# Turning normalized blocks on TensorE in a layer of sliding-window attention and routed experts

## The chip, the cores and the metric

The kernel runs on one core of one Trainium2 chip. The core has four engines that compute: TensorE (PE in the profile, its weight loads PEld), VectorE (DVE), ScalarE (ACT) and GpSimd (POOL). SyncE (SP) issues nearly all transfers, and 16 DMA engines carry them. The metric is the device time of one execution in microseconds (us), as the median of several runs.

## The reference

One transformer layer on 2048 tokens of 512 features, all in float32. A layer norm goes ahead of attention (32 heads of 16 features, each query sees the last 256 keys), a second one ahead of a mixture of 8 experts, of which each token uses two. Cut to what matters:

```python
def _A_ref(x, wqkv, wo):                    # H = 32, Dh = 16, W = 256
    q, k, v = split_heads(x @ wqkv)
    scores = einsum("bhqd,bhkd->bhqk", q, k) * (Dh ** -0.5)
    mask = (i - j >= 0) & (i - j < W)
    p = softmax(where(mask, scores, -1e9))
    return merge_heads(einsum("bhqk,bhkd->bhqd", p, v)) @ wo

def _B_ref(x, wg, w1, w2):                  # E = 8, F = 1376, K = 2
    gates = softmax(x @ wg); the two largest, scaled to sum 1 -> cw
    h = gelu(einsum("nd,edf->nef", x, w1))
    return einsum("ne,ned->nd", cw, einsum("nef,efd->ned", h, w2))

h  = x + _A_ref(layernorm(x), wqkv, wo)
h2 = h + _B_ref(layernorm(h), wg, w1, w2)
```

## The kernel before

The tokens are worked in four chunks of 512 (c = 0 to 3), each of four blocks of 128. Matrix products run in a split form: each float32 operand becomes a high part (a cast on ScalarE, line 361) and a low part (source minus high part, on VectorE, line 363, or GpSimd, line 365), and three products are added up (high by high, high by low, low by high).

For each chunk `norm_and_v` normalizes the four blocks, turns them so that features lie on partitions (the tiles `xh`, `xl`), and makes V (line 482). `qk` makes queries and keys for 8 groups of 4 heads (u = 8c + g, line 535), splits the result, writes it to DRAM (`qkd`, lines 547 to 549) and reads it back in another layout (lines 555 and 560). `maxes` computes scores for the row maxima (lines 588 to 606; the maxima go through DRAM as `md`, lines 609 and 612), and `attend` the probabilities (lines 636 to 660) and their product with V (line 676). `project` scales and projects (line 748), adds the residual (line 815), normalizes again (lines 806 and 822), writes the normalized rows to `xnd` in DRAM and computes gate logits (line 851); `route` picks two experts per token and scatters table entries. Then `experts` runs the 8 experts (lines 1118 and 1139) from about 665 us on.

How a block is turned is what the change touches. TensorE turns 128 x 128 pieces through an identity, four per block, into one PSUM bank: for chunk 0 ahead of Q, K and V (line 466), for the last chunk ahead of the gate (line 839), and in the experts (line 1090). For chunks 1 to 3 ahead of Q, K and V, and for chunks 0 to 2 ahead of the gate, the kernel goes another way: normalized rows are written to DRAM (`xd`, line 450, or `xnd`, which is written anyway), read back with 32 x 32 pieces arranged by partition (line 454 into `xz`, line 829 into `oz`), and VectorE transposes inside 32 x 32 squares (lines 472 and 844). In that form the features stand in another order, so the weights `wqkv` are loaded in the same order by `rows_of`, whose DRAM pattern has the slowest dimension 4, then 32 rows, then the columns (lines 392 and 387), and the gate weights exist twice (`wgt[0]`, `wgt[1]`).

The order on each engine is not that of the code. Each piece of work is a task of a planner (`Plan`) with an engine, a planned duration, a priority (about the number of the group it belongs to) and buffers; `Plan.order` walks through a planned time and emits the tasks, and each engine then runs its instructions strictly in that order, waiting where one is not ready. SP too issues its transfers in one row. There are 7 PSUM banks for general use (`single`, printed as one_74 to one_80 in the instruction order, `one` in the trace); `mr`, `mf` and `zone` are large SBUF tiles in which nearly all named pieces lie.

Of the kernel before, what the change touches and what calls it, by code (L numbers as in the profile page):

```python
# [155 lines left out]
def layer(tc, x, wqkv, wo, wg, w1, w2, out):  # L156
# [55 lines left out]
    xt_t = [take(mf, 512) for _ in range(2)]  # L212
# [70 lines left out]
    wgt = [const([128, 4, E], F32, f"wgt{i}") for i in range(2)]  # L283
# [61 lines left out]
    def rows_of(w, c, cols=slice(None)):  # L345
# [7 lines left out]
                     h=NH, n=NN, nt=1, xt=2, y=2, osl=1, ohl=2, ahead=2))  # L353
# [51 lines left out]
    def norm_and_v(c):  # L405
# [6 lines left out]
        zb = []  # L412
# [23 lines left out]
        for b in range(4):  # L436
            def norm(b=b):
                t = xn[xb[b].h]
                if c == 0:
                    nc.vector.tensor_scalar(xt_t[zb[b].h].rearrange("p (c q i) -> p c q i", c=4, q=4),  # L440
                                            t.rearrange("p (q c i) -> p c q i", c=4, q=4),
                                            mv["v"][:, b, 0:1], mv["y"][:, b:b + 1], op0=OP.subtract, op1=OP.mult)
                else:
                    nc.vector.tensor_scalar(t, t, mv["v"][:, b, 0:1], mv["y"][:, b:b + 1], op0=OP.subtract, op1=OP.mult)
            if c == 0:
                zb.append(Buf("xt"))
                nb.append(add("DVE", 456, norm, [rs[b]], p + 0.5, [xb[b], zb[b]]))
# [9 lines left out]
        xT, vd = [], []
        for b in range(4):
            pp = p + 1.0 + b * 0.2
            s = slice(b * 128, (b + 1) * 128)  # L460
            if c == 0:
                bk = Buf("one")

                def turn(b=b, bk=bk):
                    for k in range(4):
                        nc.tensor.transpose(single[bk.h][:, k * 128:(k + 1) * 128], xt_t[zb[b].h][:, k * 128:(k + 1) * 128], ident)
                tr = add("PE", 872, turn, [nb[b]], pp, [zb[b], bk])
                xT += split(pp, lambda s=s: xh[:, :, s], lambda s=s: xl[:, :, s],
                            lambda bk=bk: single[bk.h].rearrange("p (k t) -> p k t", k=4), [tr], [bk])
            else:  # L470
                tb = Buf("xt")
# [807 lines left out]
```

## Time and profile before

| | |
|---|---|
| median of 3 runs | 1244.97 us (1242.53 to 1249.09) |
| the profiled execution, its own time | 1246.75 us |
| span of its trace, first to last instruction | 1244.7 us |
| TensorE busy | 1118.5 us, 90% of the span |
| VectorE, ScalarE, GpSimd busy | 678.2, 540.8, 455.1 us |
| granted TensorE clock, mean | 0.948 of full speed |

Busy time is the union of an engine's instructions, so that an engine can be busy all the time with short overlaps and still not stream at its peak. The granted clock is the share of its full 2.4 GHz that TensorE was given; 0.5 is 1.2 GHz. Three stretches have to be read apart: 0 to 40 us, in which TensorE does almost nothing but turn four blocks; 40 to 705 us, the attention and routing of four chunks; and 705 us to the end, the experts, in which TensorE is busy nearly without a gap.

### The profile page before, as it was taken

To read this page: it belongs to the slowest core of one execution; us is meant where nothing else is said; L and a number is where in the kernel's file an instruction comes from. 1 tells how busy PE (TensorE), PEld (TensorE's weight loads), DVE (VectorE), ACT (ScalarE), POOL (GpSimd) and SP (SyncE) were. 2 spreads that over 40 slices of the span, in tenths; PEclk is the share of its full clock that TensorE was granted. 3 is DMA by queue.
4 is the path that set the end of the run, shared out by engine and by line. 5 is a ranking of instruction groups with operands and counts; after the bars stand their busy time and mean duration, and the time that the engine had idled before them with its cause. 6 is when DMAs were issued, how large, how long until landed. Compare 5 with 4: busy or idle time off the path is not lost.

```text
span 1244.7 us, 19621 instructions
## 1 busy us (share of the span) xinstructions
PE 1118.5 (90%) x6801; PEld 892.2 (72%) x6801; DVE 678.2 (54%) x1833; ACT 540.8 (43%) x1153; POOL 455.1 (37%) x668
## 2 busy tenths in 40 slices
PE   1797989979898999998788999999999999999994
PEld 0574666657666676766357889889798897989893
DVE  4288567977787786776546144434243342434341
ACT  1335555434554445544555245425253351626240
POOL 4734544744556464653844411220302112020101
PEclk9998998999899898996887899999999999999997
DMA  3489799884799758777332634442534334353422
GB/s 114 112 239 274 207 243 275 252 197 89 190 260 263 179 120 213 197 214 183 108 118 75 144 104 123 113 82 89 120 115 122 87 107 87 105 130 112 105 66 29
DMA packets 111617, 185.51 MB, mean 149 GB/s; under 512 B 25092, under 2 KB 44612, under 8 KB 111508
## 3 DMA queue, kind: packets, MB, share of 16 engines
q1 hardware_dynamic: 102852, 166.42, 47.7%
q0 software_dynamic: 8656, 17.73, 7.7%
q8 instruction: 56, 0.92, 0.3%
q14 instruction: 53, 0.43, 0.1%
HBM read 124.51 MB, written 59.60 MB: 148 GB/s over the span
## 4 chain that ended last, share of the span: by engine, by line
PE 67%; DMA 17%; DVE 6%; SPq 3%; POOL 2%; issue 2%; ACT 1%; POOLq 0%; DVEq 0%; ACTq 0%
PE one L1139 21%; PE one L1118 21%; PE one L588 5%; PE one L535 5%; PE oT L676 4%; PE one L636 4%; DMA mr<-qkd 3%; PE one L748 2%; PE one L482 2%; DMA md<-mt 2%; DMA mr<-md 2%; DMA od<-zone 1%; PE one L851 1%; SPq L387 1%; DVE mx L597 1%
## 5 line engine op out<-in xcount | busy, mean ns | idle before, releaser
L640 ACT ACTIVATE zone<-one 128x384 f32<-128x384 f32 (+1 forms) x480 | 207.8, 494 | 155.2 <-PE one L636 131.7
L1118 PE MATMUL one<-mr 128*128 128x256 f32 (+7 forms) x1980 | 269.2, 298 | 0.0
L1118 PEld LDWEIGHTS one<-mr 128*128 128x128 f32 (+1 forms) x1980 | 266.7, 188 | 1.1
L1139 PE MATMUL one<-zone,mr 128*128 128x512 f32 (+3 forms) x1080 | 260.4, 397 | 0.0
L660 POOL TENSOR_SCALAR_AFFINE_SELECT zone<-zone 128x256 f32<-128x256 f32 (+1 forms) x368 | 169.5, 483 | 201.4 <-ACT zone L640 198.8
L1139 PEld LDWEIGHTS one<-zone,mr 128*128 128x128 f32 (+3 forms) x1080 | 193.3, 181 | 53.0
L363 DVE TENSOR_TENSOR mr<-one,mr 128x256 fp32r<-128x256 f32 (+9 forms) x205 | 100.5, 494 | 180.1 <-ACT mr L361 171.2
L597 DVE TENSOR_REDUCE mx<-one 128x1 f32<-128x256 f32 (+2 forms) x472 | 192.3, 426 | 0.8
L588 PE MATMUL one<-mr 126*128 126x384 f32 (+2 forms) x512 | 166.1, 376 | 19.9 <-DMA mr<-qkd 10.7
L636 PE MATMUL one<-mr 128*128 128x384 f32 (+1 forms) x592 | 152.9, 336 | 21.1 <-DMA mr<-md 11.2
L594 DVE COPY_PREDICATED one<-above,one 128x128 f32<-128x128 uint32 x448 | 120.8, 289 | 77.3 <-PE one L588 68.7
L588 PEld LDWEIGHTS one<-mr 126*128 126x128 f32 x512 | 95.7, 201 | 78.1 <-issue 25.9
L636 PEld LDWEIGHTS one<-mr 128*128 128x128 f32 x592 | 109.6, 204 | 48.6 <-DVE mx L597 17.0
L361 ACT CAST mr<-one 128x256 fp32r<-128x256 f32 (+9 forms) x205 | 87.6, 431 | 128.8 <-PE one L1090 113.6
L1085 POOL DMA_INDIRECT mf<-xnd,tb x36 | 35.1, 975 | 287.6 <-PE one L1090 271.4
L535 PE MATMUL one<-mr 128*128 128x512 f32 x384 | 108.8, 413 | 23.2 <-ACT mr L361 23.0
L361 ACT CAST mr<-mf 128x512 fp32r<-128x512 f32 (+4 forms) x120 | 93.2, 787 | 82.2 <-DMA mf<-in_B_w_dram 26.1
L1123 ACT ACTIVATE one<-one 128x256 f32<-128x256 f32 (+7 forms) x165 | 65.2, 395 | 142.7 <-PE one L1118 132.6
L1145 DVE TENSOR_SCALAR mf<-one,tb 128x512 f32<-128x512 f32 (+3 forms) x36 | 27.0, 750 | 173.2 <-PE one L1139 173.2
L1147 POOL DMA_INDIRECT out_dram<-mf,tb x36 | 61.5, 1708 | 162.2 <-DVE mf L1145 142.6
L676 PE MATMUL oT<-zone 128*17 128x384 f32 (+2 forms) x1408 | 110.9, 407 | 8.1 <-POOL zone L660 6.9
L365 POOL TENSOR_TENSOR mr<-mf,mr 128x512 fp32r<-128x512 f32 (+2 forms) x74 | 94.1, 1284 | 55.4 <-ACT mr L361 50.6
(141 smaller groups left out, 965.6 us busy)
## 6 DMA issues: line engine op xcount, KB each, us to landing
mf<-in_B_w_dram SPq DMA_DIRECT2D x32, 688.0 KB
mf<-in_B_w_dram SPq DMA_DIRECT2D x40, 512.0 KB
qkd<-mr SPq DMA_DIRECT2D x32, 512.0 KB
mr<-qkd SPq DMA_DIRECT2D x80, 192.0 KB
mr<-qkd SPq DMA_DIRECT2D x48, 288.0 KB
mr<-wgd SPq DMA_DIRECT2D x24, 512.0 KB
mf<-in_A_x_dram SPq DMA_DIRECT2D x32, 256.0 KB
qkd<-mr SPq DMA_DIRECT2D x64, 128.0 KB
```

Source lines behind the costliest of these rows:

```text
L361: a = add("ACT", 51 + n * 0.86, lambda: nc.scalar.copy(dst_h(), src()), deps, prio, bufs)
L363: b = add("DVE", 65 + n * 1.05, lambda: nc.vector.tensor_sub(dst_l(), src(), f32(dst_h())), [a], prio, bufs)
L535: nc.tensor.matmul(single[bk.h], wt()[:, int(i == 1), k * 128:(k + 1) * 128], xt[:, k], start=(i == 0 and k == 0), stop=(i == 2 and k == 3))
L588: nc.tensor.matmul(view()[:, j], Q[slot.h][0:126, h + j, b * 128:(b + 1) * 128], K[slot.h][0:126, (h + j) // 2, (b + k0) * 128:(b + 3) * 1 ...
L594: nc.vector.copy_predicated(t[:, :, n - 128:n], above.unsqueeze(1).to_broadcast([128, m, 128]), src)
L597: nc.vector.tensor_reduce(mx_t[slot.h][:, h:h + m, b], view()[:, :, max(0, n - 256):n], axis=AX.X, op=OP.max)
L636: nc.tensor.matmul(single[bk.h][:, off:off + w], K[slot.h][:, h // 2, r * 128:(r + 1) * 128], Q[slot.h][:, h:h + hs, b * 128:(b + m) * 128 ...
L640: return add("ACT", 51 + n * 0.833, lambda: nc.scalar.activation(dst(), single[bk.h][:, 0:n].rearrange(order, q=128, **({"h": 2} if "h" in ...
L660: nc.gpsimd.affine_select(v, v, pattern=[[0, v.shape[1]], [-1 if far else 1, 128]], compare_op=OP.is_gt if far else OP.is_ge, fill=0.0, ba ...
L676: nc.tensor.matmul(oT[32 * j:32 * j + 17, b * 128:(b + n) * 128], V[blk % NV][:, 4 * g + j, :], PT[pt.h][j // 2][:, off:off + n, j % 2], s ...
L1118: nc.tensor.matmul(bank(), a[:, k, f * 128:f * 128 + w], b[:, k, :n], start=(i == 0), stop=(i == 11))
L1139: nc.tensor.matmul(single[bk.h][:n], h[a][:w], spot["w2"][b][f][:w], start=(f == 0 and q == 0), stop=(f == NF - 1 and q == 2))
```

## The change

All blocks are now turned by TensorE, out of the normalized tile itself: chunks 1 to 3 ahead of Q, K and V (line 454 of the new kernel; for chunk 0 it was so), and chunks 0 to 2 ahead of the gate (line 811). The bounces through `xd` and back from `xnd`, and the 32 x 32 transposes, are gone. After a turn the high part is cast out of PSUM on ScalarE, as before, and the low part comes from VectorE, not GpSimd; ahead of the gate ScalarE copies the turned block to `nt_t`. The features keep their order, so `wqkv` is loaded as plain blocks of 128 rows. The columns for the first four groups of Q and K (half 0) are loaded first, then those of V, then half 1. There is one `wgt`. The priority of the gate's turn is now that of its block, not of the chunk.

```diff
-    wqk_in = [dma(lambda k=k: nc.sync.dma_start(wqk[:, k], rows_of(wqkv, k, slice(0, 1024))), 524288, [], -9) for k in range(4)]
+    wqkv_rows = wqkv.rearrange("(k p) n -> p k n", p=128)
+    def wqk_half(k, i):
+        def cols(a):
+            return a.rearrange("p (s i n) -> p s i n", s=2, i=2)[:, :, i]
+        nc.sync.dma_start(cols(wqk[:, k]), cols(wqkv_rows[:, k, 0:1024]))
+    wqk_in = [[dma(lambda k=k, i=i: wqk_half(k, i), 262144, [], -9 if i == 0 else -2.9) for k in range(4)] for i in range(2)]
     for k in range(4):
-        load_split(k, rows_of(wqkv, k, slice(1024, 1536)), (wvh, wvl), k, -3, wv_done, "POOL" if k < 4 else "DVE")
+        load_split(k, wqkv_rows[:, k, 1024:1536], (wvh, wvl), k, -3, wv_done, "POOL")
...
-                a = add("DVE", 456, norm, rs, p + 0.5, [xb[b]])
-                nb.append(dma(lambda b=b: nc.sync.dma_start(xd[c][b * 128:(b + 1) * 128], xn[xb[b].h]), 262144, [a], p + 0.5, [xb[b]]))
-        if c > 0:
-            zr = []
-            for f in range(4):
-                zr.append(dma(lambda f=f: nc.sync.dma_start(
-                    xz[f * 32:(f + 1) * 32].rearrange("p (t c) -> p t c", c=128),
-                    ap(xd[c], f * 128, [[512, 32], [16384, 16], [1, 128]])), 262144, nb, p + 0.6, xb))
+                nc.vector.tensor_scalar(t, t, mv["v"][:, b, 0:1], mv["y"][:, b:b + 1], op0=OP.subtract, op1=OP.mult)
+            nb.append(add("DVE", 456, norm, [rs[b] if c == 0 else rs[0]], p + 0.5, [xb[b]]))
...
-                tr = add("DVE", 610, lambda b=b, tb=tb: nc.vector.transpose(
-                    xt_t[tb.h].rearrange("p (k t j) -> p t k j", k=4, t=4),
-                    xz[:, b * 512:(b + 1) * 512].rearrange("p (t k i) -> p t k i", t=4, k=4)), zr, pp, xb + [tb])
-                xT += split(pp, lambda s=s: xh[:, :, s], lambda s=s: xl[:, :, s], lambda tb=tb: xt_t[tb.h].rearrange("p (k t) -> p k t", k=4),
-                            [tr] + free_x, [tb], lo="POOL")
+            bk = Buf("one")
+            def turn(b=b, bk=bk):
+                for k in range(4):
+                    nc.tensor.transpose(single[bk.h][:, k * 128:(k + 1) * 128], xn[xb[b].h][:, k * 128:(k + 1) * 128], ident)
+            tr = add("PE", 440, turn, [nb[b]] + free_x, pp, [xb[b], bk])
+            xT += split(pp, lambda s=s: xh[:, :, s], lambda s=s: xl[:, :, s],
+                        lambda bk=bk: single[bk.h].rearrange("p (k t) -> p k t", k=4), [tr], [bk])
...
-                      lambda: wqk.rearrange("p k (s g c) -> p k s g c", s=2, g=8)[:, :, :, g], wqk_in, wsb, lo="DVE" if g < 0 else "POOL")
+                      lambda: wqk.rearrange("p k (s g c) -> p k s g c", s=2, g=8)[:, :, :, g], wqk_in[g // 4], wsb, lo="DVE" if g < 0 else "POOL")
...
-        if not end:
-            for f in range(4):
-                zr.append(dma(lambda f=f: nc.sync.dma_start(
-                    oz[f * 32:(f + 1) * 32].rearrange("p (t c) -> p t c", c=128),
-                    ap(xnd, (512 * c + 128) * 512 + f * 128, [[512, 32], [16384, 16], [1, 128]])), 262144,
-                    [xn_done[4 * c + b] for b in range(4)], p + gap, [zs]))
...
-                cp = add("DVE", 610, lambda b=b: nc.vector.transpose(
-                    nt_t.rearrange("p k (t j) -> p t k j", t=4), oz[:, b * 512:(b + 1) * 512].rearrange("p (t k i) -> p t k i", t=4, k=4)),
-                    zr, pb, [zs, tb])
+            pb = p + 0.7 + 0.3 * b if end else p + step * b + 0.9
+            tb, bk = Buf("nt"), Buf("one")
+            def turn(bk=bk, nb=nbs[b]):
+                for k in range(4):
+                    nc.tensor.transpose(single[bk.h][:, k * 128:(k + 1) * 128], n_t[nb.h][:, k * 128:(k + 1) * 128], ident)
+            tr = add("PE", 440, turn, [norms[b]], pb, [bk, nbs[b]])
+            cp = add("ACT", 478, lambda bk=bk: nc.scalar.copy(nt_t, single[bk.h].rearrange("p (k t) -> p k t", k=4)), [tr], pb, [bk, tb])
```

ScalarE at the start, before. `one_74` is the bank of the first turned block, the `mf` sources are columns of Q and K weights, the `zone` sources the V weights.

```order
L361 CAST mr<-one_74 128x4x128
L361 CAST mr<-mf 128x512 x2
L361 CAST mr<-zone 128x512 x2
L361 CAST mr<-one_75 128x4x128
L361 CAST mr<-zone 128x512
L361 CAST mr<-one_76 128x4x128
L361 CAST mr<-zone 128x512
L361 CAST mr<-one_77 128x4x128
L361 CAST mr<-mf 128x512 x6
```

Each turned block stood behind one more piece of V weights. ScalarE at the start, now:

```order
L360 CAST mr<-mf 128x512 x2
L360 CAST mr<-zone 128x512 x2
L360 CAST mr<-one_74 128x4x128
L360 CAST mr<-zone 128x512 x2
L360 CAST mr<-mf 128x512 x2
L360 CAST mr<-one_75 128x4x128
L360 CAST mr<-one_76 128x4x128
L360 CAST mr<-one_77 128x4x128
L360 CAST mr<-mf 128x512 x4
```

The casts of the first four groups' weights and of V now stand ahead of the last three blocks.

GpSimd at the start, now: low parts of weights (`mf` for Q and K, `zone` for V), zeroing of the Q and K tiles (lines 406 and 407) and of a column in the V tiles (408); the two low parts at the end hold that of the first group's queries and keys.

```order
L364 TENSOR_TENSOR mr<-mf,mr 128x512
L406 MEMSET mr 128x2048
L407 MEMSET mr 128x1536
L364 TENSOR_TENSOR mr<-mf,mr 128x512
L364 TENSOR_TENSOR mr<-zone,mr 128x512 x3
L364 TENSOR_TENSOR mr<-mf,mr 128x512
L364 TENSOR_TENSOR mr<-zone,mr 128x512
L406 MEMSET mr 128x2048
L408 MEMSET zone 128x32 x10
L407 MEMSET mr 128x1536
L364 TENSOR_TENSOR mr<-mf,mr 128x512 x2
```

Of these rows the second pair of 406 and 407 and the row of 408 stood behind the first group's low part before.

TensorE at the first gate of chunk 0, before; L851 is the gate's product, which reads what VectorE transposed.

```order
L588 MATMUL one_77<-mr 128x384
L482 MATMUL one_76<-mr 128x512 x4
L851 MATMUL one_75<-wgt_118,mf 128x8 x4
L588 MATMUL one_79<-mr 128x384
L588 MATMUL one_80<-mr 128x384
L588 MATMUL one_74<-mr 128x384
L676 MATMUL oT<-zone 17x384 x4
L851 MATMUL one_78<-wgt_118,mf 128x8 x4
```

The same gate now, from the second block's projection (L727) to the first block's turn (L811). L567 and L615 are scores (588 and 636 before), L655 the product with V.

```order
L727 MATMUL one_76<-mr 128x512 x12
L567 MATMUL one_78<-mr 128x384
L567 MATMUL one_80<-mr 128x384
L567 MATMUL one_77<-mr 128x384
L655 MATMUL oT<-zone 17x256 x4
L655 MATMUL oT<-zone 17x128 x4
L615 MATMUL one_74<-mr 128x384
L615 MATMUL one_75<-mr 128x384
L615 MATMUL one_74<-mr 128x384
L615 MATMUL one_76<-mr 128x384
L615 MATMUL one_75<-mr 128x384
L811 MATMUL one_74<-ident,mf 128x128 x4
```

The turn stands eleven rows behind the first block's own projection, ahead of the third block's projection; before, all four gates came after all four projections and after the read from DRAM.

## Rows read from the trace of the kernel before

**Rows 1.** The page, part 1: busy us, share of the span, instructions.
```profile
PE 1118.5 (90%) x6801; PEld 892.2 (72%) x6801; DVE 678.2 (54%) x1833; ACT 540.8 (43%) x1153; POOL 455.1 (37%) x668
```
**Rows 2.** Windows: stretch, length, busy by engine, granted clock, DMA share, GB/s.
```profile
40.00:705.00 665.00, 590.48 (x3698) 426.20 (x3699) 457.82 (x1458) 320.67 (x698) 349.12 (x585) 0.92 0.72 191
```
**Rows 3.** Windows at the start: loads of x, then of weights.
```profile
2.00:4.00 2.00, 0.00 (x0) 0.00 (x0) 2.00 (x2) 0.10 (x1) 2.00 (x2) 1.00 0.98 309
20.00:25.00 5.00, 0.00 (x0) 0.00 (x0) 0.00 (x0) 0.00 (x0) 0.00 (x0) 1.00 0.26 106
```
**Rows 4.** Timeline of SP's issues at the start: start, us, line, tile, count.
```profile
2.69 6.00 SPq L392 DMA_DIRECT2D mf<-in_A_wqkv_dram  x4
8.73 18.67 SPq L387 DMA_DIRECT2D zone<-in_A_wqkv_dram  x4
```
**Rows 5.** Timeline of the other engines at the start; brackets: idle before, releaser.
```profile
6.81 0.69 DVE L417 BATCH_NORM_STATS2 s<-mf 128x6 f32<-128x512 f32 x1 [0.59 <-DMA mf<-in_A_x_dram]
...
28.29 1.14 ACT L361 CAST mr<-mf 128x512 fp32r<-128x512 f32 x2 [16.72 <-DMA mf<-in_A_wqkv_dram]
...
39.97 7.26 PE L535 MATMUL one<-mr 128*128 128x512 f32 x24 [23.00 <-ACT mr L361]
...
45.84 1.29 POOL L365 TENSOR_TENSOR mr<-mf,mr 128x512 fp32r<-128x512 f32 x1 [5.04 <-ACT mr L361]
...
47.66 1.81 POOL L400 MEMSET mr<- 128x2048 f32 x1
...
57.94 1.08 PE L588 MATMUL one<-mr 126*128 126x128 f32 x8
```
**Rows 6.** Timeline of TensorE: turns of chunk 0, and of chunk 3 with its gate.
```profile
14.10 2.87 PE L466 MATMUL one<-ident,mf 128*128 128x128 f32 x12 [3.15 <-DVE mf L440]
...
658.48 1.12 PE L839 MATMUL one<-ident,mf 128*128 128x128 f32 x4 [2.06 <-DVE mf L822]
662.01 1.88 PE L851 MATMUL one<-wgt,mf 128*128 128x8 f32 x8 [2.42 <-ACT mf L841]
```
**Rows 7.** TensorE's waits, 40 to 705 us: who, releaser, us, times, longest.
```profile
PE one L851 <- DVE mf L844: 11.3, 3, 5.4
PE one L636 <- DMA mr<-md: 11.2, 7, 3.1
PE one L588 <- DMA mr<-qkd: 10.7, 5, 2.9
...
PE one L588 <- DMA mf<-xd: 4.1, 1, 4.1
```
**Rows 8.** Timeline at the first gate of chunk 0, VectorE and TensorE.
```profile
273.90 0.71 DVE L844 STREAM_TRANSPOSE mf<-mf 128x512 f32<-128x512 f32 x1 [3.62 <-DMA md<-mt]
...
274.66 1.32 PE L851 MATMUL one<-wgt,mf 128*128 128x8 f32 x8 [3.73 <-DVE mf L844]
```
**Rows 9.** Windows behind the three gates of chunks 0, 1 and 2.
```profile
270.00:290.00 20.00, 16.27 (x74) 12.93 (x74) 9.83 (x32) 2.17 (x5) 0.67 (x3) 0.74 0.21 41
...
420.00:440.00 20.00, 17.81 (x117) 13.98 (x116) 12.68 (x43) 7.37 (x17) 4.30 (x10) 0.83 0.51 87
...
570.00:600.00 30.00, 25.32 (x147) 18.79 (x147) 20.87 (x67) 13.59 (x29) 13.38 (x23) 0.66 0.56 159
```
**Rows 10.** A window in which both bounces are under way.
```profile
250.00:260.00 10.00, 6.79 (x43) 4.30 (x42) 8.57 (x29) 3.66 (x9) 4.50 (x11) 1.00 1.05 293
```
**Rows 11.** Timeline: one block's projection, then residual to normalized rows on VectorE.
```profile
243.69 2.92 PE L748 MATMUL one<-mr 128*128 128x512 f32 x12
...
247.18 0.65 DVE L815 TENSOR_TENSOR mf<-one,mf 128x512 f32<-128x512 f32 x1
...
251.03 0.54 DVE L822 TENSOR_SCALAR mf<-mf,mvh,ryh 128x512 f32<-128x512 f32 x1
```
**Rows 12.** Groups by line, 40 to 705 us: busy us, mean ns, idle before.
```profile
L844 DVE STREAM_TRANSPOSE mf<-mf 128x512 f32<-128x512 f32 x12 | 8.5, 704 | 11.9 <-DMA mf<-xnd 8.3 <-DMA md<-mt 3.6
...
L841 ACT COPY mf<-one 128x512 f32<-128x512 f32 x4 | 2.4, 589 | 3.2 <-PE one L839 3.2
```

More of the change, by code (lines that the diff above doesn't have):

```diff
@@ L211, in layer @@
     xn = [xz[:, i * 512:(i + 1) * 512] for i in range(4)]
-    xt_t = [take(mf, 512) for _ in range(2)]
     hl_f = take(mf, 512)
@@ L282, in layer @@
     ones = const([128, 128], BF, "ones")
-    wgt = [const([128, 4, E], F32, f"wgt{i}") for i in range(2)]
+    wgt = const([128, 4, E], F32, "wgt")
     tok = const([128, 16], I32, "tok")
@@ L352, in layer @@
     plan = Plan(dict(xn=4, wgs=2, hl=1, qk=NQ, pt=NPT, osb=1, one=7, mx=3, ab=3, oT=1,
-                     h=NH, n=NN, nt=1, xt=2, y=2, osl=1, ohl=2, ahead=2))
+                     h=NH, n=NN, nt=1, y=2, osl=1, ohl=2, ahead=2))
     add = plan.add
@@ L411, in norm_and_v @@
         mv = dict(v=mv_t[c % 2], y=ry_t[c % 2])
-        zb = []
         st = []
@@ L460, in norm_and_v @@
             s = slice(b * 128, (b + 1) * 128)
[L461 to L471, printed above, removed]
-                tr = add("DVE", 610, lambda b=b, tb=tb: nc.vector.transpose(
-                    xt_t[tb.h].rearrange("p (k t j) -> p t k j", k=4, t=4),
-                    xz[:, b * 512:(b + 1) * 512].rearrange("p (t k i) -> p t k i", t=4, k=4)), zr, pp, xb + [tb])
-                xT += split(pp, lambda s=s: xh[:, :, s], lambda s=s: xl[:, :, s], lambda tb=tb: xt_t[tb.h].rearrange("p (k t) -> p k t", k=4),
-                            [tr] + free_x, [tb], lo="POOL")
+            bk = Buf("one")
[5 more added lines that the diff above has]
+                        lambda bk=bk: single[bk.h].rearrange("p (k t) -> p k t", k=4), [tr], [bk])
             d = xT[-2:] + wv_done
@@ L507, in later @@
             dma(lambda: nc.sync.dma_start(out[0:128], zero), 262144, made2 + after, 1.0),
-            dma(lambda: nc.sync.dma_start(wgt[0], wg.rearrange("(k p) e -> p k e", p=128)), 16384, after, 1.0)])
-        init.extend(dma(lambda q=q: nc.sync.dma_start(
-            wgt[1][q * 32:(q + 1) * 32], wg[q * 128:(q + 1) * 128].rearrange("(c i) e -> i c e", i=32)), 4096, after, 1.0) for q in range(4))
+            dma(lambda: nc.sync.dma_start(wgt, wg.rearrange("(k p) e -> p k e", p=128)), 16384, after, 1.0)])
     init, keep = [], []
@@ L825, in project @@
                                      [norms[b]], pb + 0.6, [nb])
-        zr, zs = [], Buf("osl")
-        if not end:
-            for f in range(4):
-                zr.append(dma(lambda f=f: nc.sync.dma_start(
-                    oz[f * 32:(f + 1) * 32].rearrange("p (t c) -> p t c", c=128),
-                    ap(xnd, (512 * c + 128) * 512 + f * 128, [[512, 32], [16384, 16], [1, 128]])), 262144,
-                    [xn_done[4 * c + b] for b in range(4)], p + gap, [zs]))
-        for b in range(4):
-            pb = p + 0.7 + 0.3 * b if end else p + gap + 0.5 + 0.2 * b
-            tb, bk = Buf("nt"), Buf("oT" if 0 else "one")
-            if end:
-                def turn(bk=bk, nb=nbs[b]):
-                    for k in range(4):
-                        nc.tensor.transpose((oT if 0 else single[bk.h])[:, k * 128:(k + 1) * 128], n_t[nb.h][:, k * 128:(k + 1) * 128], ident)
-                tr = add("PE", 872, turn, [norms[b]], pb, [bk, nbs[b]])
-                cp = add("ACT", 478, lambda bk=bk: nc.scalar.copy(nt_t, (oT if 0 else single[bk.h]).rearrange("p (k t) -> p k t", k=4)),
-                         [tr], pb, [bk, tb])
-            else:
-                cp = add("DVE", 610, lambda b=b: nc.vector.transpose(
-                    nt_t.rearrange("p k (t j) -> p t k j", t=4), oz[:, b * 512:(b + 1) * 512].rearrange("p (t k i) -> p t k i", t=4, k=4)),
-                    zr, pb, [zs, tb])
+        for b in range(4):
+            pb = p + 0.7 + 0.3 * b if end else p + step * b + 0.9
[5 more added lines that the diff above has]
+            cp = add("ACT", 478, lambda bk=bk: nc.scalar.copy(nt_t, single[bk.h].rearrange("p (k t) -> p k t", k=4)), [tr], pb, [bk, tb])
             bk = Buf("one")
@@ L850, in gate @@
                 for k in range(4):
-                    nc.tensor.matmul(single[bk.h][:, 0:E], nt_t[:, k], wgt[0 if end else 1][:, k], start=(k == 0), stop=(k == 3))
+                    nc.tensor.matmul(single[bk.h][:, 0:E], nt_t[:, k], wgt[:, k], start=(k == 0), stop=(k == 3))
             gm = add("PE", 756, gate, [cp] + init, pb, [bk, tb])
```

10 lines of the change are left out of this document (removed).

## The prediction

> **What bounds the kernel now.** I read the page first, then the windows, then TensorE's waits. The page says that TensorE is busy for 90% of the span [rows 1], but that is a mean over three stages. From 705 us to the end the experts run, which the change leaves alone. From 40 to 705 us TensorE is busy for 590.5 of 665 us at a mean granted clock of 0.92, VectorE for 458 us, and the DMA engines for 0.72 of the time [rows 2]: no engine is full, TensorE is nearest, and 74.5 us of idle time lie in between. From 0 to 40 us TensorE waits for data: its first matmul of Q and K starts at 39.97 us after 23 us of idling, released by ScalarE, which had itself waited 16.72 us for the weights [rows 5]. So there are two questions: what the start is worth, and whether turns on TensorE cost more between 40 and 705 us than the bounces that they replace.
>
> **The start.** The loads of x run at a DMA share of 0.98 and 309 GB/s, the weight loads behind them at a share of 0.26 and 106 GB/s, for more than 20 us [rows 3]. SP is held up too: four issues take 6.00 us for the columns of Q and K and 18.67 us for those of V [rows 4]. A share of 0.26 is four engines of sixteen, and the slowest dimension in the DRAM pattern of these loads is 4; x comes as blocks of 128 rows, and so do the new loads. The Trainium skill (DMA: Bandwidth & Descriptors, Rules for kernel authors) says that a transfer whose outermost dimension is smaller than 16 is confined to at most that many engines; the trace agrees with 0.26. By this rule the new loads, whose slowest dimension is 128 rows, use all sixteen.
>
> The third block of x is there at 6.81 us [rows 5], so let x be in by 6.8. Of the new loads, the first half of Q and K is 1.05 MB, V as much: 3.4 us each at 309 GB/s, in at about 10.2 and 13.6 us, the second half at 17.0. ScalarE then has 12 casts ahead of the first matmul (first order rows of the change), at 1.14 / 2, some 0.6 us each: 10.5 + 7.2 = 17.7 us in place of 39.97. But the first scores need more: the low part of the first group's Q and K on GpSimd, then the trip through DRAM. GpSimd starts at about 11 us and has ahead of it seven splits of weights at 1.29 us, four memsets at no more than 1.81 us and ten small ones (some 0.7 us); then its own 1.29 us [rows 5]: 11 + 9.0 + 7.2 + 0.7 + 1.3 = 29.2 us, against 45.84 + 1.29 = 47.1 before. That is 18 us earlier; scores stood at 57.94 us before [rows 5] and should start near 40. Ends: 22 us if the first matmul decides, 13 us if the first group's low part is the second of its pair (1.3 us) and the 12 V matmuls that now come after the first scores (12 x 7.26 / 24 = 3.6 us [rows 5]) are paid in full. I take **-17 us**, nearest to GpSimd's rows.
>
> **Turns on TensorE.** New are 12 blocks ahead of Q, K and V and 12 ahead of the gate, four turns each: 96 instructions. Twelve took 2.87 us in a row [rows 6], 0.24 us each: 96 x 0.24 = 23 us of TensorE work. The lower end is 0, if all of it falls into the 74.5 us of idle time; the upper is 27 us, at the 1.12 us that four took standing alone [rows 6]. TensorE is busy for 0.89 of this stretch [rows 2], but its busy time holds overlap, so I take 0.8 of 23: **+18 us**. The Trainium skill (TensorE: Matmul & The Clock Gate, Part 4: PE-mode transpose) gives about 275 ns for a turn inside a kernel, which would be 26 us and, by the same 0.8, a sum 3 us higher; the trace has 240 ns, and I go by it.
>
> VectorE loses 24 transposes of 0.70 us [rows 12] and takes 12 low parts of about the same length; ScalarE gets 12 copies of 0.59 us [rows 12], GpSimd loses 12 splits of 1.29 us. VectorE is busy for 69% of the stretch, ScalarE for 48%, GpSimd for 52% [rows 2]; these changes I cost at nothing. Cover gone, ScalarE's would cost 7 us.
>
> **The gate's bounce.** The gate waits three times for VectorE's transpose, 11.3 us in all [rows 7]. At the first one VectorE had been idle for 3.62 us in front of the transpose [rows 8], with the work on row maxima queued behind it; the releaser named there is another transfer, but what the transpose reads is the block from DRAM. The whole core runs dry: from 270 to 290 us ScalarE is busy for 2.2 us, and TensorE's granted clock is 0.74, from 420 to 440 us 0.83, from 570 to 600 us 0.66 [rows 9]. A mean of 0.74 over 20 us is 10.4 us at half speed, which costs 5.2 us of work; in the same way 3.4 and 10.2 us, 18.8 in all. The waits go (**-11 us**), and of the lost clock I take half (**-9 us**; ends 0 and -18.8), since other short waits stand nearby.
>
> **The other bounce.** Scores waited 4.1 us for `xd` [rows 7]; with what VectorE lost in front of its transposes I take **-5 us** (ends -2 and -8). Both bounces together are 36 transfers of 0.26 MB, 9.4 MB, and fall into stretches in which the DMA engines are full: 1.05 and 293 GB/s from 250 to 260 us [rows 10]. At that rate they take 32 us of all engines. What it is worth stands in TensorE's waits for `md` and `qkd`, 11.2 and 10.7 us [rows 7]: ends 0 and -22, I take a third, **-7 us**.
>
> **New waits.** A turn now waits on TensorE for the normalized block, and the gate for ScalarE's copy; whatever stands behind them in TensorE's row (scores, the products with V) waits too, and VectorE and ScalarE with it. One block's way on VectorE from residual to normalized rows took 247.18 to 251.57, 4.4 us [rows 11]. In the new order eleven rows stand between a block's projection and its turn, among them the second block's projection, 2.9 us [rows 11], and 16 scores and products with V, which at the stretch's mean of 590.5 / 3698 = 0.16 us [rows 2] are 2.6 us: 5.5 us, a little more than the 4.4. In chunk 3, where turns stand so today, the first one waited 2.06 us and its gate 2.42 us [rows 6]. I take one wait of 2 us per chunk, **+6 us**; ends 0, and 54 us for 12 x (2.06 + 2.42).
>
> **Sum.** -17 + 18 - 11 - 9 - 5 - 7 + 6 = -25 us. The profiled execution took 1246.75 us, 1.8 above the median: 1221.8 there, and **1220 us** as a median.
>
> **Rivals.**
> 1. *The turns are nearly free.* If TensorE's busy time is mostly latency, 96 turns cost 5 us and the DMA relief is worth 15: -25 - 13 - 8 = -46 us, 1199 us. For it speaks that no engine is full [rows 2]; against it that TensorE's work is rowed strictly.
> 2. *The start is given back.* DMA engines and VectorE could hold chunk 0 to its old pace, so that of 17 us only 2 stay: 1235 us. For it: shares above 1 soon after [rows 10]; against it: those transfers start earlier as well.
> 3. *Slower: TensorE stands in front of each turn.* The place is the row from projection to turn. If every block paid 2.06 + 2.42 us, 54 in place of 6, the sum is +23 us, 1268 us. It decides once the mean wait for a block is above 2.6 us (25 + 6 = 31 us over 12 blocks). Against it: VectorE's 4.4 us lie under the 5.5 us of cover.
> 4. *The change does not do what it says at the start.* If the halves, which have a middle dimension of two pieces per row, were spread by that one, they would run on two engines, at 53 GB/s; 1.05 MB would take 20 us, and the 17 us would be lost: 1237 us. The slowest dimension is 128, as in the loads of x, so I give it little.
>
> **How the numbers follow.** Forecast 0.60 (1206 to 1236 by its terms), rival 1: 0.18, rival 2: 0.08, rival 3: 0.10, rival 4: 0.04. The range, **1198 to 1240 us**, takes in the forecast, rivals 2 and 4 and about half of rival 1; rival 3 and the rest stay out. A measurement of this kernel can tell about 0.5%, 6.2 us, from no change: faster means below 1238.7. The forecast nearly all, rival 1 and half of rivals 2 and 4 lie there: faster 0.82; within 0.5% 0.08; slower 0.10.
>
> **What would show it.** Right: a DMA share near 1 until some 17 us and none of 0.26; the first Q and K matmul near 18 us and the first scores near 40; SP's eight weight issues without a stall; no wait of the gate for VectorE; a higher granted clock behind the gates; TensorE's busy time between start and experts up by no more than 23 us; the experts' stretch as long as before (540 us). Wrong: waits of the turns for VectorE or of the gate for ScalarE that sum to over 20 us; a wait for `qkd` right after the start as long as what was won; a clock no higher than 0.92 from the first scores to the experts.

## The result, and the profile after

The changed kernel took 1209.57 us as a median of four runs (1208.27 to 1211.77), the kernel before 1244.61 us beside it: a ratio of 0.9728 (95% interval 0.97 to 0.9757). The profiled execution took 1208.33 us with a span of 1206.1 us, against 1246.75 and 1244.7. A second series of six runs of the same kernel, beside the last experiments, gave 1204.87 us (1200.54 to 1208.81); over all ten runs the median is 1208.1 us, and that is what the experiments are compared with. The two medians of one and the same kernel lie 4.7 us apart, so differences of under some 5 us can't be told from scatter. The traces of the two series are two executions of the same program, and the second one (`after_again`) shows below which readings of the first hold. Of the six runs of `whole_again` below, two are left out of its median, for they lay over 1.5% above its fastest, in a slower state.

The page's first part, and TensorE's waits from 18 to 670 us (engine, instruction, releaser, us, times, longest), answer to [rows 1] and [rows 7]:

```profile
PE 1116.0 (93%) x6897; PEld 891.1 (74%) x6897; DVE 662.7 (55%) x1821; ACT 544.2 (45%) x1165; POOL 441.7 (37%) x656
```

```profile
PE one L615 <- DMA mr<-md: 13.2, 6, 5.2
PE one L567 <- DMA mr<-qkd: 12.8, 7, 3.0
...
PE one L818 <- ACT mf L813: 2.2, 2, 1.3
...
PE one L811 <- DVE mvh L378: 1.9, 2, 1.1
...
PE one L811 <- DVE mf L801: 1.0, 1, 1.0
```

96 instructions more on TensorE, and it is busy for 2.5 us less. The waits for VectorE at the gate (11.3 us) and for `xd` (4.1 us) are gone; those of the turns (L811) and of the gate for ScalarE's copy (L818) come to 5.1 us. Of these, 3.4 us stand in chunk 3, where TensorE turned the blocks before too and such waits came to 4.8 us, the two of [rows 6] among them; the new waits of chunks 0 to 2 are 1.7 us. Chunk 3 in the changed kernel:

```profile
620.96 0.66 PE L811 MATMUL one<-ident,mf 128*128 128x128 f32 x4 [0.99 <-DVE mf L801]
622.95 1.83 PE L818 MATMUL one<-wgt,mf 128*128 128x8 f32 x8 [1.33 <-ACT mf L813]
625.91 1.12 PE L811 MATMUL one<-ident,mf 128*128 128x128 f32 x4 [1.12 <-DVE mvh L378]
```

The waits for `md` and `qkd`, 21.9 us before, did not shrink: 26.0 us, and 25.3 in the second trace.

The start. SP's issues, the DMA share while the loads run, ScalarE's first instructions, then the first matmul of Q and K, the first group's low part and the first scores, as in [rows 3 to 5]:

```profile
2.69 1.97 SPq L397 DMA_DIRECT2D mf<-in_A_wqkv_dram  x4
4.70 2.60 SPq L386 DMA_DIRECT2D zone<-in_A_wqkv_dram  x4
8.52 2.52 SPq L397 DMA_DIRECT2D mf<-in_A_wqkv_dram  x4
```

```profile
2.00:14.00 12.00, 3.01 (x13) 2.61 (x14) 10.20 (x37) 3.24 (x5) 8.70 (x9) 1.00 0.98 328
```

```profile
10.74 1.28 ACT L360 ACT_TABLE_LOAD   x1 [10.74 <-DMA mf<-in_A_wqkv_dram]
...
12.04 1.14 ACT L360 CAST mr<-mf 128x512 fp32r<-128x512 f32 x2
```

```profile
18.29 7.35 PE L514 MATMUL one<-mr 128*128 128x512 f32 x24 [3.36 <-ACT mr L360]
...
24.24 1.28 POOL L364 TENSOR_TENSOR mr<-mf,mr 128x512 fp32r<-128x512 f32 x1 [2.14 <-ACT mr L360]
...
36.12 2.05 PE L567 MATMUL one<-mr 126*128 126x128 f32 x8 [2.23 <-DMA mr<-qkd]
```

The twelve new issues go out without a stall, and the first scores stand at 36.12 us in place of 57.94.

To see where the 38.6 us between the two spans went, I cut both traces at the same work: the first scores, the end of the last products of V of chunks 1, 2 and 3, and the first long run of experts. First the kernel before, then the changed one (stretch, length, busy by engine, granted clock, DMA share, GB/s):

```profile
0.00:58.00 58.00, 22.02 (x89) 17.77 (x90) 18.33 (x52) 13.44 (x23) 31.28 (x46) 1.00 0.34 110
58.00:149.20 91.20, 81.40 (x467) 57.46 (x469) 70.24 (x198) 43.26 (x92) 45.27 (x69) 0.94 0.85 240
149.20:298.50 149.30, 133.30 (x841) 97.22 (x838) 113.71 (x363) 68.47 (x152) 68.70 (x117) 0.92 0.82 218
298.50:448.50 150.00, 135.75 (x909) 97.72 (x909) 112.25 (x370) 75.11 (x166) 81.98 (x140) 0.94 0.78 203
448.50:705.50 257.00, 222.54 (x1420) 159.56 (x1419) 157.92 (x517) 127.42 (x278) 140.99 (x236) 0.88 0.59 155
```

```profile
0.00:36.10 36.10, 19.54 (x76) 15.39 (x77) 16.78 (x52) 13.73 (x24) 29.86 (x45) 0.95 0.59 175
36.10:128.70 92.60, 87.06 (x494) 64.02 (x498) 72.64 (x199) 42.13 (x91) 41.62 (x66) 0.91 0.73 216
128.70:268.70 140.00, 130.99 (x873) 95.12 (x869) 108.04 (x359) 70.68 (x157) 64.98 (x116) 0.98 0.76 209
268.70:417.70 149.00, 138.11 (x941) 100.19 (x940) 107.63 (x365) 76.22 (x169) 78.78 (x140) 0.95 0.69 183
417.70:666.50 248.80, 216.27 (x1433) 152.50 (x1431) 151.62 (x512) 129.20 (x282) 137.30 (x231) 0.93 0.58 155
```

The second column is the length. The start gives 21.9 us, the stretch with the gate of chunk 0 gives 9.3 and that with the gate of chunk 2 gives 8.2. That with the gate of chunk 1 gives 1.0, and the second stretch is 1.4 us longer. The experts take 540 us in both. Of the start's 21.9 us some 3.6 are work that was moved and not saved: the 12 V matmuls that the prediction names now stand behind the first scores. And a stretch of one trace is one execution. In the second trace of the same kernel the first and the third stretch read

```profile
0.00:35.90 35.90, 20.75 (x77) 16.52 (x77) 16.09 (x51) 13.72 (x24) 29.59 (x45) 1.00 0.58 174
...
126.90:273.00 146.10, 133.75 (x873) 97.92 (x869) 111.00 (x359) 71.17 (x156) 64.78 (x116) 0.94 0.72 200
```

so that chunk 0's gate gives 3.2 us there and not 9.3. Chunk 2's, at 247.5 us, gives 9.5.

### The profile page after: what moved, and what is told of

Read it like the earlier page. It is cut to its first block, busy times and chain, and to the rows that moved or that the text cites. A ratio compares the mean times of both kernels' runs of the same rounds, so it can differ in the third digit from the quotient of the medians.

```text
span 1206.1 us, 19807 instructions
## 1 busy us (share of the span) xinstructions
PE 1116.0 (93%) x6897; PEld 891.1 (74%) x6897; DVE 662.7 (55%) x1821; ACT 544.2 (45%) x1165; POOL 441.7 (37%) x656
## 5 line engine op out<-in xcount | busy, mean ns | idle before, releaser
L567 PE MATMUL one<-mr 126*128 126x384 f32 (+2 forms) x512 | 167.6, 368 | 19.1 <-DMA mr<-qkd 12.8
L362 DVE TENSOR_TENSOR mr<-one,mr 128x256 fp32r<-128x256 f32 (+9 forms) x217 | 108.8, 505 | 129.0 <-ACT mr L360 128.5
L615 PE MATMUL one<-mr 128*128 128x384 f32 (+1 forms) x592 | 158.9, 335 | 17.0 <-DMA mr<-md 13.2
L567 PEld LDWEIGHTS one<-mr 126*128 126x128 f32 x512 | 95.1, 197 | 74.2 <-issue 25.0
L360 ACT CAST mr<-one 128x256 fp32r<-128x256 f32 (+9 forms) x217 | 94.4, 439 | 118.5 <-PE one L1057 113.5
L615 PEld LDWEIGHTS one<-mr 128*128 128x128 f32 x592 | 108.6, 198 | 44.8 <-issue 15.9
L655 PE MATMUL oT<-zone 128*17 128x384 f32 (+2 forms) x1408 | 109.6, 401 | 7.8 <-POOL zone L639 7.5
L360 ACT CAST mr<-mf 128x512 fp32r<-128x512 f32 (+4 forms) x108 | 86.0, 808 | 64.5 <-DMA mf<-in_B_w_dram 28.1
L364 POOL TENSOR_TENSOR mr<-mf,mr 128x512 fp32r<-128x512 f32 (+3 forms) x62 | 79.1, 1284 | 39.2 <-ACT mr L360 34.9
```

What stands on the lines that cost most here:

```text
L360: a = add("ACT", 51 + n * 0.86, lambda: nc.scalar.copy(dst_h(), src()), deps, prio, bufs)
L362: b = add("DVE", 65 + n * 1.05, lambda: nc.vector.tensor_sub(dst_l(), src(), f32(dst_h())), [a], prio, bufs)
L567: nc.tensor.matmul(view()[:, j], Q[slot.h][0:126, h + j, b * 128:(b + 1) * 128], K[slot.h][0:126, (h + j) // 2, (b + k0) * 128:(b + 3) * 1 ...
L615: nc.tensor.matmul(single[bk.h][:, off:off + w], K[slot.h][:, h // 2, r * 128:(r + 1) * 128], Q[slot.h][:, h:h + hs, b * 128:(b + m) * 128 ...
L655: nc.tensor.matmul(oT[32 * j:32 * j + 17, b * 128:(b + n) * 128], V[blk % NV][:, 4 * g + j, :], PT[pt.h][j // 2][:, off:off + n, j % 2], s ...
```

## The experiments

| kernel | median, us (runs) | ratio to before, 95% interval |
|---|---|---|
| changed kernel, all runs | 1208.1 (10) | 0.9728 (0.97–0.9757), then 0.9667 (0.9637–0.9697) |
| `slow_start` | 1226.26 (4) | 0.9867 (0.9799–0.9935) |
| `gate_bounce` | 1227.25 (4) | 0.9872 (0.9799–0.9944) |
| `gate_alone` | 1227.36 (10) | 0.989 (0.9852–0.9928) |
| `turns_twice` | 1217.85 (4) | 0.9779 (0.9701–0.9858) |
| `dma_load` | 1212.29 (6) | 0.9766 (0.9725–0.9807) |
| `gate_warm` | 1225.52 (6) | 0.9868 (0.9829–0.9907) |
| `whole_blocks`, `whole_again` | 1201.12 (6), 1204.57 (4) | 0.9671 (0.9634–0.9709), 0.964 (0.9595–0.9684) |
| `halves_warm` | 1205.64 (6) | 0.9691 (0.9652–0.973) |
| `filled` | 1206.43 (6) | 0.9712 (0.968–0.9744) |
| `whole_filled` | 1200.22 (6) | 0.9638 (0.9606–0.967) |

The intervals are 8 to 10 us either way for `slow_start`, `gate_bounce` and `turns_twice`, some 4 to 6 us for the other experiments.

**The start undone** (`slow_start`).

```diff
-        load_split(k, wqkv_rows[:, k, 1024:1536], (wvh, wvl), k, -3, wv_done, "POOL")
+        load_split(k, rows_of(wqkv, k, slice(1024, 1536)), (wvh, wvl), k, -3, wv_done, "POOL" if k < 4 else "DVE")
```

and the columns of Q and K in the same way.

> The changed kernel with its start undone: the weights of Q, K and V come in the old way (whole blocks, slowest dimension 4), everything behind the start stays as changed. Features are then permuted again, so VectorE writes the normalized rows in the permuted order into two buffers of their own. Theory (the start is worth its own lead and the lead stays to the end): first scores back near 58 us from 36.1, total 17 to 22 us above the changed kernel, 1227 to 1232 us. Rival (the start is given back by DMA and VectorE in chunk 0): the total rises by 2 to 5 us only, 1212 to 1215 us, and the first V of chunk 1 still starts near 110 us.

1226.26 us, 18 above the changed kernel. Its first scores:

```profile
54.09 1.16 PE L562 MATMUL one<-mr 126*128 126x128 f32 x8 [2.05 <-issue]
```

They stand 18.0 us later, not the 22 that would bring them back to 58 us, since here too only 24 V matmuls stand ahead of them, against 36 in the kernel before. The same cuts as above stand 17.0, 21.2, 22.3 and 20.8 us later. The lead of the start is carried to the end; that it is given back falls.

**The gate's part, undone and alone** (`gate_bounce`, `gate_alone`): the diff's last piece taken out of the changed kernel, and put by itself into the kernel before.

> The changed kernel with the gate part undone alone: the normalized rows of chunks 0 to 2 go through DRAM and VectorE's 32x32 transposes to the gate, as before. Theory by the sum of the prediction: waits 11 and lost clock 9 come back, half of the turns (9), half of the new waits (3) go, half of the DMA relief (3.5) is lost: 11 us slower, about 1221 us, and TensorE waits for VectorE's transpose near 11 us in sum. Rival (turns nearly free, relief 15): turns give back 2.5 only and the relief costs 7.5: 25 us slower, about 1235 us.

> The kernel before with the gate part alone: the 12 blocks of chunks 0 to 2 are turned on TensorE ahead of the gate, start and features of Q, K and V as before. Theory by the sum: 11 us faster than the kernel before, about 1233 us. Rival (turns nearly free): 25 us faster, about 1220 us. The distance from this kernel to the one with the slow start is what the turns of x on TensorE are worth: theory +3 us (they cost 9 + 3 and give back 5 + 3.5), rival -10 us.

Undone it costs 19.2 us (1227.25 against 1208.1), alone it brings 17.5 (1227.36 against 1244.85), more than the 11 of the sum and less than the rival's 25. The kernel with the slow start differs from `gate_alone` by the turns of x, and by the order at the start (its first matmul of Q and K comes at 33.46 us, that of `gate_alone` at 38.68): 1226.26 against 1227.36. So that part is worth about 1 us, with an interval of nearly 10 us either way: nothing that this measurement can tell, and not told from the theory's +3 either. Start, gate and x are three steps of a path from one kernel to the other, so that they add up says nothing; that the gate's part is worth about the same at either end does. Both kernels move two things at once, the hop through DRAM and the gate's place in TensorE's row (block by block now, all four behind the last projection before); which of the two costs, no run separates. In `gate_bounce` TensorE's wait is back, and two of its stretches (the same cuts) show in which form:

```profile
PE one L832 <- DVE mf L825: 14.7, 3, 6.7
```

```profile
130.60:278.10 147.50, 130.93 (x858) 95.44 (x858) 112.33 (x363) 68.47 (x152) 65.55 (x116) 0.95 0.76 205
...
429.20:688.10 258.90, 224.06 (x1419) 160.87 (x1418) 155.98 (x517) 127.80 (x278) 140.75 (x235) 0.86 0.59 153
```

Around the gate of chunk 2 the stretch is 10.1 us longer than in the changed kernel, and 7.8 of them are busy time, at a granted clock of 0.86 in place of 0.93: no more work, at a lower clock. Around that of chunk 0 the busy time is that of the changed kernel (130.99) and the stretch 7.5 us longer: idling. Against the second trace of the changed kernel it is 1.4 us longer only, so this one is not clear. In the ten traces here with turned gates and each turn issued once, the stretch of chunk 2's gate takes 244.3 to 251.2 us, in the three with the bounce 254.1 to 258.9; for chunk 0's it is 137.9 to 146.1 against 146.6 to 149.3, and for chunk 1's, 143.9 to 156.2 against 150.0 to 151.1, there is no difference to be seen.

**Each new turn twice** (`turns_twice`).

```diff
-                for k in range(4):
+                for k in [0, 1, 2, 3] * (2 if c else 1):
                     nc.tensor.transpose(single[bk.h][:, k * 128:(k + 1) * 128], xn[xb[b].h][:, k * 128:(k + 1) * 128], ident)
```

and in the same way the turns ahead of the gate, where the chunk is not the last.

> The changed kernel with each of the 96 new turns issued twice into the same place: 96 turns more on TensorE, nothing else. Theory (a turn costs 0.24 us, 0.8 of it on the path): 18 us slower, about 1228 us, TensorE's busy time 18 to 23 us higher. Rival (turns lie in gaps or are mostly latency): 5 us slower or less, 1210 to 1215 us.

9.8 us for 96 turns more, 0.10 us each: between the two. But the interval overlaps that of the changed kernel, and the four runs reach from 1207.15 to 1220.09 us, so the time alone decides for neither. The busy time tells more. The groups by line (busy us, mean ns, idle before), first here, then in the changed kernel:

```profile
L454 PE MATMUL one<-ident,mf 128*128 128x128 f32 x112 | 17.0, 296 | 14.2 <-DVE mf L444 14.2
...
L811 PE MATMUL one<-ident,mf 128*128 128x128 f32 x112 | 16.1, 286 | 2.9 <-DVE mvh L378 1.9 <-DVE mf L801 0.8 <-ACT zone L619 0.2
```

```profile
L454 PE MATMUL one<-ident,mf 128*128 128x128 f32 x64 | 11.4, 315 | 11.0 <-DVE mf L444 11.0
L811 PE MATMUL one<-ident,mf 128*128 128x128 f32 x64 | 10.5, 288 | 2.9 <-DVE mvh L378 1.9 <-DVE mf L801 1.0
```

96 turns more make 11.2 us of busy time (33.1 against 21.9). The mean of one, near 290 ns, is not its price: turns in a row overlap. In the middle of the changed kernel four turns take 0.60 us; in chunk 3 of the kernel before four took 1.12, and twelve at the start 2.87 [rows 6]. The row of 0.60 and the granted clock around it, then the clock around that of 1.12 in the kernel before:

```profile
228.90 0.60 PE L811 MATMUL one<-ident,mf 128*128 128x128 f32 x4
```

```profile
228.00:230.00 2.00, 2.00 (x17) 1.72 (x13) 1.97 (x4) 1.02 (x3) 0.08 (x1) 1.00 0.98 275
```

```profile
655.00:660.00 5.00, 2.53 (x7) 1.20 (x6) 4.76 (x14) 1.17 (x3) 3.61 (x4) 0.50 0.61 216
```

So the 1.12 us are a price at 1.2 GHz, the 0.60 us one at 2.4 GHz.

**The traffic of the bounces put back** (`dma_load`).

> The changed kernel with the traffic of both bounces put back and nobody waiting for it: 12 writes of the normalized rows of x and 24 reads in pieces of 512 bytes (half of them into unused memory of the core, half into DRAM), 36 transfers of 0.26 MB at their old places in SP's queue. Theory (DMA relief is worth 7 us): about 1217 us, with TensorE's waits for md and qkd 7 us above the changed kernel's 26. Rival (relief worth 15): 1225 us. Third (the transfers lay beside other work and cost nothing): 1208 to 1212 us.

1212.29 us, 4 above. By the ratios to the kernel before it is 5 to 12 us, depending on which series of the changed kernel stands beside it; the interval overlaps that of the first series and not that of the second. So the forecast's 7 us are not excluded, and the rival's 15 lie above all of these. TensorE's waits for the two transfers come to 28.2 us, against 26.0 and 25.3 in the two traces of the changed kernel:

```profile
PE one L631 <- DMA mr<-md: 14.7, 8, 3.2
...
PE one L583 <- DMA mr<-qkd: 13.5, 6, 3.6
```

**The gate's wait filled with turns of the identity** (`gate_warm`).

```diff
+                for _ in range((22, 10, 16, 0)[c] if b == 0 else 0):
+                    nc.tensor.transpose(single[bk.h][:, 0:128], ident, ident)
```

> The kernel gate_bounce (gate through DRAM again) with 22, 10 and 16 turns of the identity on TensorE ahead of the first gate of chunks 0, 1 and 2, into the gate's own bank, where TensorE waited 6.7, 3.3 and 4.7 us for VectorE's transpose. The wait stays, the idling goes. Theory (of the gate's worth of 17.7 us, about half is lost clock): the granted clock behind the gates stays near 1.00 and the time falls by 6 to 9 us from gate_bounce's 1227 to 1218 to 1221 us. Rival (behind the gates the other engines are dry, so a slower clock costs nothing): no change, 1225 to 1229 us.

No change that can be told: 1225.52 against 1227.25. The stretches behind the gates, first of `gate_bounce`, then filled:

```profile
247.00:267.00 20.00, 13.32 (x68) 10.88 (x67) 9.71 (x30) 2.78 (x6) 1.53 (x4) 0.83 0.39 71
400.00:420.00 20.00, 16.70 (x103) 13.78 (x95) 11.73 (x40) 3.81 (x9) 1.53 (x4) 0.91 0.38 68
547.00:577.00 30.00, 25.10 (x135) 17.43 (x135) 18.18 (x61) 11.85 (x25) 11.86 (x23) 0.60 0.61 169
```

```profile
244.00:264.00 20.00, 17.53 (x114) 14.02 (x113) 11.41 (x38) 2.92 (x6) 1.53 (x4) 0.91 0.42 78
396.00:416.00 20.00, 17.99 (x110) 14.14 (x108) 11.65 (x40) 3.14 (x7) 1.53 (x4) 0.91 0.41 73
540.00:570.00 30.00, 23.39 (x165) 16.69 (x165) 20.60 (x64) 12.38 (x27) 13.15 (x24) 0.79 0.71 182
```

Counted as the prediction did, the lost clock falls from 17.2 us of work (3.4, 1.8 and 12) to 9.9. The clock came back in part only; 2.0 to 3.7 us of wait were left behind the filling. Of 7.3 us kept, 1.7 show in the medians, less than the scatter, while in the two traces the stretch of chunk 2's gate is 4.9 us shorter with the filling (254.07 against 258.93 us); so how much of a lower clock behind such a wait is paid stays open.

**Whole blocks in place of halves** (`whole_blocks`, then `whole_again` beside the changed kernel, `after_again`).

```diff
-    wqk_in = [[dma(lambda k=k, i=i: wqk_half(k, i), 262144, [], -9 if i == 0 else -2.9) for k in range(4)] for i in range(2)]
+    wqk_in = [[dma(lambda k=k: nc.sync.dma_start(wqk[:, k], wqkv_rows[:, k, 0:1024]), 524288, [], -9) for k in range(4)]] * 2
```

> The changed kernel with the columns of Q and K loaded as four whole blocks of 0.52 MB ahead of V, not as halves around V; TensorE's order is the same. Theory (the first half alone lets the first matmul start): the first Q and K matmul moves from 18.3 to about 21.7 us (1.05 MB more at 309 GB/s) and the total by 3 us to about 1213 us. Rival (the casts on ScalarE and the low parts on GpSimd set the start, not the landing): first scores within 1 us of 36.1, total 1209 to 1211 us.

The first matmul of Q and K moves by 1.1 us, the first scores by 0.5:

```profile
19.37 7.39 PE L514 MATMUL one<-mr 128*128 128x512 f32 x24 [0.67 <-ACT mr L360]
...
36.58 1.16 PE L567 MATMUL one<-mr 126*128 126x128 f32 x8 [1.54 <-issue]
```

So the order of the loads is not what sets the start. The median of 1201.12 us, 7 to 8 below the changed kernel, was a surprise, and my reading of it was wrong. The changed kernel shows a granted clock of 0.86 and 0.71 from 16 to 24 us, behind a hole of 3.36 us, and 0.50 from 36 to 40; whole blocks show 1.00 in all of them. I took the clock for the cause, and ran three kernels more:

> The changed kernel once more, as a mark beside the three that follow. If the 8 us by which whole blocks were faster are theirs, it stands at 1207 to 1212 us and whole blocks at 1198 to 1204 us; if they are scatter between rounds, the two come within 3 us of one another.

> The changed kernel with whole blocks for Q and K, once more beside the changed kernel itself. Theory (the halves cost time: they open a hole of 3.4 us on TensorE ahead of the first matmul of Q and K, after which the clock is lower at the start): again 6 to 10 us below the changed kernel. Rival (scatter): within 3 us of it.

> The changed kernel with its halves, and with turns of the identity on TensorE in the two holes of the start: 12 ahead of the first matmul of Q and K (hole 3.36 us), 7 ahead of the first scores (hole 2.23 us). Waits stay, idling goes. Theory (halves cost through the clock): the granted clock from 18 to 44 us stays at 1.00 and the time falls to that of whole blocks, 1200 to 1204 us. Rival (a clock lost at the start is given back by chunk 0's later waits, as with filled): within 3 us of the changed kernel.

1204.87, 1204.57 and 1205.64 us: no difference between the three. In `halves_warm`, with turns in both holes, the granted clock reads 1.00 from 16 to 44 us:

```profile
17.54 2.77 PE L513 MATMUL one<-ident 128*128 128x128 f32 x12
...
34.89 0.93 PE L569 MATMUL one<-ident 128*128 128x128 f32 x7
```

But it reads 1.00 there in the second trace of the changed kernel too, with nothing in the holes (3.14 us ahead of the first matmul of Q and K): the lower clock of the first trace is that of one execution, not of the halves. Scatter it was, and the halves are worth nothing that can be measured here.

**The holes of the start filled with work** (`filled`, and with whole blocks `whole_filled`).

```diff
-            rds.append(dma(rk, 294912, dep, p + 0.6, [slot]))
+            rds.append(dma(rk, 294912 + (400000 if u == 0 else 0), dep, p + 0.6, [slot]))
...
-        sp = split(p + 0.2, ..., [cp], [hb], lo="POOL")
+        sp = split(p + 0.2, ..., [cp], [hb], lo="DVE" if u == 0 else "POOL")
```

> The changed kernel with two edits at the start: the low part of the first group's Q and K is made by VectorE in place of GpSimd, and the planner is told that the first group's read from DRAM takes longer, so that 8 products of V stand on TensorE ahead of the first scores, where it waited 2.2 us and ran at a granted clock of 0.50 right after. Theory (the wait and the clock behind it are paid in full): 4 us faster, about 1205.5 us. Rival (chunk 0 waits for row maxima and DMA soon after in any case): within 1 us, 1208.5 to 1210.5 us.

> Whole blocks together with both edits of filled: the low part of the first group on VectorE, 8 products of V ahead of the first scores. Theory (both gains are of the start and not the same hole): 2 to 3 us below whole blocks, 1198 to 1200 us. Rival (chunk 0 waits for row maxima in either case): within 1.5 us of whole blocks.

In `whole_filled` the number added to the size is 200000, which gives the same 8 products ahead. `filled` is at 1206.43 us, within scatter of the changed kernel. Its first scores start without a wait and at full clock, and then:

```profile
68.00:72.00 4.00, 1.44 (x8) 0.96 (x6) 3.96 (x12) 0.00 (x0) 0.00 (x0) 1.00 1.04 300
72.00:76.00 4.00, 0.90 (x3) 0.82 (x3) 0.96 (x3) 0.14 (x1) 0.00 (x0) 0.68 1.03 278
```

TensorE is busy for 2.3 of 8 us while the DMA engines are full; in the two traces of the changed kernel it is 6.5 and 5.2. That what was won is given back there fits these rows, but one execution shows it. `whole_filled`, at 1200.22 us, has the lowest median of its series, 4.7 us below the changed kernel beside it, but the intervals overlap (0.9606 to 0.967 and 0.9637 to 0.9697): whether it is faster stays open.

## Why the prediction was right, point by point

The time, 1209.57 us, lies in the range and inside the forecast's own 1206 to 1236, 10 us below the number. The terms one by one:

- **Start, -17**: right in size, 18 us by `slow_start`, but by another path than the sum took. The first matmul of Q and K came at 18.29 us (17.7 forecast), in part by luck: ScalarE's first cast came at 12.04 us, not at 10.5, behind a table load of 1.28 us that the sum left out, and the twelve casts then took 6.2 us, not 7.2. For the first scores I went by GpSimd's rows and put the first group's low part behind all splits of V, done at 29.2 us. It is the row at 24.24, ahead of the last split and of the last zeroing rows (not the last two rows of GpSimd's order, as the section on the change says), and was done at 25.5 us. GpSimd had idled for 2.14 us ahead of it, waiting for ScalarE, so the first matmul decided, the end of 22 us: the first scores came at 36.12, not near 40. Less the 3.6 us of V matmuls that now come behind them, the lead of 21.8 us is 18.2. The Trainium skill (DMA: Bandwidth & Descriptors, Rules for kernel authors) on transfers with a short outermost dimension is borne out: with 128 rows outermost the loads ran at a DMA share of 0.98 and 328 GB/s from 2 to 14 us, with 4 at 0.26 and 106 GB/s [rows 3]. SP's issues shrank with it, from 6.00 and 18.67 us [rows 4] to 1.97 to 2.60.
- **Turns on TensorE, +18**: this is the step that was mis-sized. I took 0.24 us for a turn from [rows 6], a row of the start, and 0.8 of it as paid. The turns that were added run in the middle, where four take 0.60 us at a granted clock of 1.00: 24 groups are 14.4 us of work, the second 96 turns added 11.2 us of busy time, and by the medians they cost 9.8 us. The 275 ns of the Trainium skill (TensorE: Matmul & The Clock Gate, Part 4: PE-mode transpose), given there for bf16, are near the mean duration of one of these float32 turns, 288 and 315 ns; as a price per turn in a row, the measurement of 0.10 to 0.15 us decides.
- **Gate's bounce, waits -11**: right in place. The wait is gone; 14.7 us came back when the bounce was put back. The gate's part as a whole was worth 17.5 to 19.2 us, where its terms add up to 11.
- **Lost clock, -9**: the clock rose behind the gates as said, from 0.74, 0.83 and 0.66 [rows 9] to 1.00, 0.83 and 0.89:

```profile
214.00:234.00 20.00, 18.77 (x129) 14.72 (x129) 15.79 (x62) 9.48 (x22) 12.14 (x18) 1.00 0.70 212
356.00:376.00 20.00, 18.50 (x100) 14.26 (x100) 11.63 (x45) 7.90 (x17) 10.83 (x15) 0.83 0.67 231
500.00:530.00 30.00, 27.67 (x177) 20.29 (x175) 18.46 (x66) 12.75 (x29) 14.02 (x22) 0.89 0.77 205
```

  That is 12.1 of the 18.8 us of work; in the second trace, in 20, 20 and 30 us from the same turns on, the clock is 1.00 in all three. What it is worth by itself was not shown: 7.8 us of busy time in one stretch of `gate_bounce` speak for it, `gate_warm` does not.
- **The other bounce, -5, and its half of the turns**: near nothing together, as the terms said (-5, +9, half of the waits and of the relief: +3.5 against a measured -1, which may be off by nearly 10).
- **DMA relief, -7**: 4 us by the medians, 5 to 12 by the ratios, so neither shown nor refuted. The place I named was wrong: the waits for `md` and `qkd` did not shrink at all.
- **New waits, +6**: sized too large. Of the 5.1 us, 3.4 are in chunk 3, where the turns stood already; chunks 0 to 2, for which I had taken 2 us each, have 1.7 in all. No block of theirs waits for more than 0.9 us in one place, so the slower rival's 2.6 us per block was never near.

So the likeliest case came true, 10 us better than its sum. By the medians 8 us of that are the turns and 4 the new waits, less some 3 us of relief; since neither the turns' 9.8 us nor the relief is clear of scatter and the lost clock was not priced by itself, this division is an estimate, and that the sum came as near as it did is partly errors that cancel. The first rival had the direction (turns cheap), but a relief of 15 us did not show; the start was not given back (rival 2), and the halves ran on all engines (rival 4: 0.98 in place of two engines' share). The experts' 540 us stayed. One sign came true in part only: the DMA share is near 1 until 14 us, not 17, since the twelve loads are nearly all in by then.

## What to carry to other kernels

Price an operation from rows of the stretch where it will run, and read the granted clock beside the row: four turns took 1.12 us at 0.50 and 0.60 us at 1.00. A hop through DRAM, late in the row, ahead of a small product can hold one engine's row while the others run dry; here taking away three such places was worth half of the gain, most clearly at the third, and the 9.4 MB of both bounces with nobody waiting 4 to 12 us. Before explaining a difference of a few us, run the kernel that it is measured against once more beside it, and trace it once more too: one stretch of the same kernel took 140.0 and 146.1 us.

## What was not expected of the hardware

The row of the granted clock doesn't tell everything at the start of the program. The 12 turns of the identity at 17.54 us took 0.23 us each, in a stretch whose granted clock reads 1.00; 22 of them in the middle of `gate_warm`, behind steady work, took 0.12 us each:

```profile
247.15 2.59 PE L832 MATMUL one<-ident 128*128 128x128 f32 x22
```

A ratio of two is that of the two clock levels, 1.2 and 2.4 GHz, so I read the start as run at the lower one; no row shows it. The second trace of the changed kernel points the same way: its first 24 matmuls of Q and K take 8.63 us and the 24 of V behind them 5.60, both at a granted clock of 1.00.

And two executions of one program differ in their clock. From 16 to 24 us the first trace of the changed kernel reads 0.86 and 0.71 and from 36 to 40 us 0.50, the second 1.00 throughout, behind holes of 3.36 and 3.14 us. The two executions took 1208.33 and 1207.89 us. So the lower clock of the first trace is not the price of the earlier start, and it left nothing that these times show.
